# A one-core attention and token-MLP kernel: the first four tiles alone before the first scores, K projected tile by tile, and later slots for the layernorm, FFN and output projection

## The chip, the cores and the metric

The kernel runs on one core of one Trainium2 chip. The metric is device time in microseconds (us) of one execution; lower is better. Engines are named as in the profile: PE is TensorE (matmuls; PEld its weight loads), DVE is VectorE, ACT is ScalarE, POOL is GpSimd, SP is SyncE, which issues the transfers.

## The reference

An input x of 2048 tokens by 512 goes through a layernorm; on it run a multi-head attention (32 heads of 16) and a token-mixing MLP, which mixes over the 2048 tokens with a hidden size of 1376 and has a layernorm of its own. The output is the sum of both and of x.

```python
def _A_ref(x, wqkv, wo):                      # x is layernormed
    qkv = (x @ wqkv).reshape(B, S, 3, H, Dh)  # S 2048, H 32, Dh 16
    scores = einsum("bhqd,bhkd->bhqk", q, k) * Dh ** -0.5
    p = softmax(scores, axis=-1)
    return einsum("bhqk,bhkd->bhqd", p, v) (heads merged) @ wo
def _B_ref(x, w1, b1, w2, b2):
    h = layernorm(x)
    u = gelu(einsum("bsd,sf->bdf", h, w1) + b1)
    return (einsum("bdf,fs->bds", u, w2) + b2) transposed
xn = layernorm(x)
return x + _A_ref(xn, ...) + _B_ref(xn, ...)
```

## The kernel before, in words

**Tiles and blocks.** The tokens lie in 16 tiles of 128. The attention runs in 32 blocks: four blocks of 512 queries (`qb`) by eight groups of four heads (`G`, in pairs: a slice `T` of 128 columns of Q and K and an even or odd half `e`). A block has 16 periods, one per tile of keys. In a period PE computes four score tiles of 128x512 (`score_group`, L664), which row groups of the array hold side by side; ScalarE takes two exps of 128x1024 (`exp_pair`, L673) from PSUM to SBUF as `pT`; two periods later PE multiplies V by `pT` (`pv_group`, L683). A column of ones in V (17 columns per head in the tile `V17`) gives the softmax denominators. At the end of a block `epilogue_copy` (L604) and `task_epilogue_rest` take the sums from PSUM, invert them on DVE (L611, L616) and multiply on POOL (L619) into `oT`.

**Order.** The program writes the instructions of every engine in one fixed order; `Sched` derives the semaphore waits from the keys that an operation reads and writes (`add`, L69). Every engine works strictly in that order. PSUM has eight banks: 0 to 3 (later 0 to 5) hold scores, 6 (`PV_BANK`) the sums, 7 (`EX_BANK`) everything else, one job at a time. Side work gets slots of two units per period (`EXTRA_BUDGET`, L33; a 128x512 matmul is one unit): `sched_list` (L695) gives each job a first period and a rank; `kt`, `qt` and `vt` are the projections of K, Q and V for later slices, `ut` and `yt` the two FFN matmuls, `op` the output projection. Beside this queue, free tasks advance by one step each per period: `epi`, the rest of a block's epilogue, and `ln2`, the second layernorm.

**Prologue.** `pro_stage` (L441) is a pipeline over tiles. A tile goes through `ln_stats` (L326: DVE stats and aggregate, then two small POOL steps that give the inverse deviation), `ln_norm` (L339: DVE), `transpose_pe` (L353), `transpose_copy` (L360: PSUM to `xnT`), `vT_pe` and `vT_evac` (V for slice 0), and every fourth tile `kt_pe` and `kt_evac` (K for slice 0 and 512 keys). Ten stages run ahead of the first scores (`NSTG_PRE = NPRE + 3 + SH`, L465), with ACT for most evictions; the Q projection of slice 0 (`qt_proj`, L392) is in them. The other stages run one per period in block 0, all on DVE. Within a stage the order is eviction, projection, transpose copy, then norm, transpose, then stats of the next tile. `late_consts` (L314) follows the ten stages: POOL clears `wo_pad` (L316), then SP loads it. POOL's `ln_stats` steps queue behind that clear.

The places the change touches in `sched_list`:

```python
for ft in range(NFT):                                              # L704
    sched_list.append((P(1, 4) + 6 * ft, 2, "ut", ft))
for st in range(NT):
    sched_list.append((P(1, 4) + 6 * NFT + 7 * st, 3, "yt", st))
...
        sched_list.append((P(8 * (qb + 1), 8) + 4 * sti, 4, "op", (qb, sti)))
```

`P(b, kt)` is the period of block b and key tile kt.

## Time and profile before

| | |
|---|---|
| time, median of 4 runs | 1021.05 us (1020.63 to 1021.7) |
| profiled execution, its own time | 1020.83 us |
| its span on the core | 1019.0 us |
| busy: ACT / PE / DVE / POOL | 958.7 / 841.2 / 309.6 / 69.3 us |
| mean granted PE clock | 0.775 of full speed |
| chain that ended last | ACT 78%, PE 11%, DVE 7%, POOL 2%, issue 2% |

The profile's busy times are of one execution. A busy PE is not a PE at its peak, since its clock changes and matmuls overlap. Timeline rows give start and length in us from the span's start, engine, line, operation, tiles and, in brackets, the idle time before it with what ended it. Merged rows (x2, x4) show several instructions from the first's start to the last's end.

### The profile page before, as it was taken

The page shows a single profiled execution, that of the slowest core. Times are in us where ns is not written, and L with a number is a line of the kernel's source. Part 1 is how long each engine was busy: PE and PEld are TensorE (multiplying, and loading weights), DVE is VectorE, ACT ScalarE, POOL GpSimd, SP SyncE. Part 2 cuts the span into 40 slices and gives each one's busy share as a digit, 9 for nine tenths or more (in the row PEclk, how much of TensorE's full clock was granted, in tenths as well). Part 3 has the DMA queues.
Part 4 walks back from the last instruction along what each step waited for, and adds up shares of the span by engine and source line. Part 5 has one row for each costly group of instructions (what it writes and reads, how often), then busy time and mean ns, then how long its engine had stood idle before and what let it go on. Part 6 is the DMA issues. An engine that isn't in the chain of part 4 may idle for free.

```text
span 1019.0 us, 11820 instructions
## 1 busy us (share of the span) xinstructions
PE 841.2 (83%) x4957; PEld 205.5 (20%) x5024; DVE 309.6 (30%) x503; ACT 958.7 (94%) x1049; POOL 69.3 (7%) x110
## 2 busy tenths in 40 slices
PE   3786788888788878888888888898989889998986
PEld 1321231231112112212222222211111211111111
DVE  5726632233332243232122323201121321112223
ACT  2595899999999999999999999999999999999995
POOL 2403200000000000000000000000000000000000
PEclk9675998998779787989989999955555965555576
DMA  5030000101100100111100110000000000000000
GB/s 144 19 72 1 1 1 21 22 1 27 36 21 22 21 16 1 28 29 28 33 20 25 29 28 6 16 1 1 0 1 1 16 6 1 1 1 1 1 1 21
DMA packets 55429, 18.33 MB, mean 18 GB/s; under 512 B 49232, under 2 KB 55376, under 8 KB 55376
## 3 DMA queue, kind: packets, MB, share of 16 engines
q1 hardware_dynamic: 55376, 17.58, 7.3%
q8 instruction: 39, 0.64, 0.3%
q14 instruction: 14, 0.11, 0.0%
HBM read 15.47 MB, written 2.10 MB: 17 GB/s over the span
## 4 chain that ended last, share of the span: by engine, by line
ACT 78%; PE 11%; DVE 7%; POOL 2%; issue 2%; another core or an unknown queue 0%; DMA 0%; ACTq 0%; DVEq 0%
ACT pT L673 77%; PE ps L664 4%; PE ps L683 2%; DVE big L345 1%; DVE stats L330 1%; POOL mv L336 1%; PE ps L522 1%; PE ps L400 1%; PE ps L568 1%; DVE QT L408 1%; POOL mv L334 1%; PE ps L382 1%; ACT ga_sb L537 1%; PE ps L549 1%; DVE mv L332 0%
## 5 line engine op out<-in xcount | busy, mean ns | idle before, releaser
L673 ACT ACTIVATE pT<-ps 128x1024 bf16<-128x1024 f32 x1024 | 948.7, 1276 | 26.2 <-PE ps L664 23.4
L664 PE MATMUL ps<-QT,KT 32*128 32x512 bf16 x2048 | 444.2, 478 | 115.7 <-ACT pT L673 96.4
L683 PE MATMUL ps<-pT,V 128*32 128x512 bf16 x2048 | 247.7, 485 | 0.6 <-ACT pT L673 0.6
L664 PEld LDWEIGHTS ps<-QT,KT 32*128 32x128 bf16 x2048 | 92.9, 94 | 502.2 <-ACT pT L673 476.0
L604 DVE COPY OT<-ps 128x512 f32<-128x512 f32 x31 | 21.4, 691 | 325.4 <-PE ps L683 325.4
L616 DVE RECIPROCAL denb<-denb 128x128 f32<-128x128 f32 x124 | 108.6, 920 | 0.9
L619 POOL TENSOR_TENSOR oT<-OT,denb 128x512 bf16<-128x512 f32 x31 | 39.2, 1266 | 837.3 <-DVE denb L616 837.3
L683 PEld LDWEIGHTS ps<-pT,V 128*32 128x32 bf16 x2048 | 52.3, 97 | 154.2 <-issue 152.4
L522 PE MATMUL ps<-big,w1blk 128*128 128x512 bf16 (+1 forms) x158 | 56.8, 435 | 5.6 <-issue 3.7
L549 PE MATMUL ps<-gT,w2blk 128*128 128x512 bf16 (+1 forms) x160 | 54.1, 405 | 3.4 <-DVE QT L408 1.8
L554 DVE SCALAR_TENSOR_TENSOR big<-ps,x_sb 128x512 f32<-128x512 f32 x16 | 11.1, 691 | 108.1 <-PE ps L549 108.1
L568 PE MATMUL ps<-wo_pad,oT 128*128 128x512 bf16 x106 | 38.3, 436 | 3.3 <-issue 2.8
L408 DVE TENSOR_SCALAR QT<-ps,qmask 128x512 bf16<-128x512 f32 x32 | 22.5, 746 | 32.3 <-PE ps L400 30.3
L581 DVE TENSOR_TENSOR osb<-ps,big 128x512 bf16<-128x512 f32 x16 | 11.0, 688 | 58.9 <-PE ps L568 56.8
L400 PE MATMUL ps<-xnT,wqkv_sb 128*128 128x512 bf16 x55 | 24.5, 528 | 4.7 <-DVE KT L390 2.6
L382 PE MATMUL ps<-xnT,wqkv_sb 128*128 128x512 bf16 x55 | 20.7, 464 | 8.8 <-DVE KT L390 5.9
L527 DVE TENSOR_SCALAR u_sb<-ps,b1col 128x512 f32<-128x512 f32 (+1 forms) x11 | 8.2, 748 | 62.0 <-PE ps L522 62.0
L355 PE MATMUL ps<-ident,big 128*128 128x128 bf16 x64 | 8.6, 277 | 16.8 <-DVE big L345 16.7
L611 DVE STREAM_SHUFFLE denb<-OT 128x512 f32<-128x512 f32 x31 | 22.4, 721 | 0.0
L486 PE MATMUL ps<-wqkv_sb,xnT 128*128 128x128 bf16 x192 | 16.1, 232 | 6.1 <-DVE V L390 4.5
L389 ACT ACTIVATE xnT<-ps 128x512 bf16<-128x512 bf16 x8 | 4.8, 597 | 17.0 <-PE ps L355 17.0
L336 POOL TENSOR_TENSOR mv<-mv,mhalf 128x1 f32<-128x1 f32 x32 | 18.1, 567 | 2.7
(52 smaller groups left out, 213.0 us busy)
## 6 DMA issues: line engine op xcount, KB each, us to landing
w1blk<-in_B_w_dram SPq DMA_DIRECT2D x10, 512.0 KB, 4.1
w2blk<-in_B_w_dram SPq DMA_DIRECT2D x16, 320.0 KB, 3.3
out_dram<-osb SPq DMA_DIRECT2D x16, 128.0 KB, 1.7
wqkv_sb<-in_A_wqkv_dram SPq DMA_DIRECT2D x3, 512.0 KB, 6.3
x_sb<-in_A_x_dram SPq DMA_DIRECT2D x3, 512.0 KB, 7.2
wo_pad<-in_A_wo_dram SPq DMA_DIRECT2D x8, 64.0 KB, 2.0
w2blk<-in_B_w_dram SPq DMA_DIRECT2D x16, 24.0 KB, 1.7
w1blk<-in_B_w_dram SPq DMA_DIRECT2D x1, 384.0 KB, 4.0
```

The costliest lines, as they stand in the source:

```text
L336: sc.add("pool", lambda e: e.tensor_tensor(mv[:, i, 2:3], mv[:, i, 1:2], mhalf[:], ALU.pow), reads=[("mv", i), ("mhalf",)], writes=[("mv", ...
L382: sc.add("pe", lambda e, ct=ct: e.matmul(bank(bk), lhsT=wqkv_sb[:, ct, D + 128 * T: D + 128 * T + 128], rhs=xnT[:, ct, 512 * c:512 * (c + ...
L400: sc.add("pe", lambda e, ct=ct: e.matmul(bank(bk), lhsT=wqkv_sb[:, ct, 128 * T:128 * (T + 1)], rhs=xnT[:, ct, 512 * qb:512 * (qb + 1)], st ...
L408: sc.add("dve", lambda e, e_=e_, slot=slot: e.tensor_scalar(QT[:, slot, :], bank(bk), qmask[:, e_:e_ + 1], None, ALU.mult), reads=[("bank" ...
L522: sc.add("pe", lambda e, st=st: e.matmul(bank(EX_BANK)[0:m, :], lhsT=w1blk[:, slot, st, 0:m], rhs=h_sb[:, st, :], start=(st == 0), stop=(s ...
L549: sc.add("pe", lambda e, ft=ft, m=m: e.matmul(bank(EX_BANK), lhsT=w2blk[0:m, slot, ft, :], rhs=gT[0:m, ft, :], start=(ft == 0), stop=(ft = ...
L568: sc.add("pe", lambda e, G=G: e.matmul(bank(EX_BANK), lhsT=oT[:, par, G, 128 * sti:128 * (sti + 1)], rhs=wo_pad[:, G, :], start=(G == 0), ...
L616: sc.add("dve", lambda e, cs=cs: e.reciprocal(denb[:, eb, cs], denb[:, eb, cs]), reads=[("denb", eb, c)], writes=[("denb", eb, c)])
L619: sc.add("pool", lambda e: e.tensor_tensor(oT[:, qb % 2, G, :], OT32[:, eb, :], denb[:, eb, :], ALU.mult), reads=[("OT32", eb)] + [("denb" ...
L664: sc.add("pe", lambda e, r=r, bk=bk: e.matmul(bank(bk), lhsT=KT[32 * r:32 * r + 32, T, 128 * kt:128 * (kt + 1)], rhs=QT[32 * r:32 * r + 32 ...
L673: sc.add("act", lambda e: e.activation(pT[:, buf, :], ps[:, s_ * 1024:(s_ + 1) * 1024], ACTF.Exp, scale=0.25), reads=[("bank", 2 * s_), (" ...
L683: sc.add("pe", lambda e, r=r, buf=buf, off=off: e.matmul(bank(PV_BANK)[32 * r:32 * r + 32, :], lhsT=V17[:, off:off + 32], rhs=pT[:, buf, 5 ...
```

## The change

- `Sched.add`: an operation that reads a PSUM bank now also waits for earlier readers of that bank on other engines.
- The clear of all of `V17` becomes three small clears of the one head per slice that a matmul reads before it is written, one of the end, and the ones.
- `pro_stage` is longer by two steps per tile (norm one stage after stats, transpose one after norm, V two after the copy) and stats of the next tile stand ahead of the norm. Ahead of the first scores only tiles 0 to 3 go all the way (`NSTG_PRE = NPRE + 5`, `SH = 0`), tiles 4 and 5 as far as the norm. There ACT evicts the even half of Q and DVE the odd half.
- In block 0 the K projection of slice 0 is by tile: `kt_tile_pe` and `kt_tile_evac`, 128 keys each, with keys `KTt` by tile for the scores' waits.
- `task_ln2` takes three periods per tile: stats, norm, nothing.
- `ut` and `yt` start at P(4, 2) instead of P(1, 4); the first `w1` loads at P(2, 0) instead of P(0, 8), the first `w2` loads at P(7, 0) instead of P(3, 0).
- `op` of the first three query blocks starts at P(8(qb+1)+6, 2) instead of P(8(qb+1), 8), ahead of FFN jobs that have not started, with the rank of the projections.

```diff
@@ Sched.add
+            if k[0] == "bank":
+                for r in self.readers.get(k, ()):
+                    if r.eng != eng:
+                        deps.add(r)
@@ constants
-        sc.add("dve", lambda e: e.memset(V17[:, :], 0.0), writes=[("Vpad",)] + [("Vone",)] +
-               [("V", t, T) for t in range(NT) for T in range(4)])
+        for T in range(1, 4):
+            sc.add("dve", lambda e, T=T: e.memset(v17_kh[:, :, 8 * T, 0:16], 0.0),
+                   writes=[("V", t, T) for t in range(NT)])
+        sc.add("dve", lambda e: e.memset(V17[:, NKT * H * 17:], 0.0), writes=[("Vpad",)])
@@ K by tile
+        def kt_tile_pe(T, t, bk):
+            j = t % 4
+            for ct in range(NCT):
+                sc.add("pe", lambda e, ct=ct: e.matmul(
+                    bank(bk)[:, 128 * j:128 * (j + 1)], lhsT=wqkv_sb[:, ct, D + 128 * T: D + 128 * T + 128],
+                    rhs=xnT[:, ct, 128 * t:128 * (t + 1)], start=(ct == 0), stop=(ct == NCT - 1)),
+                    reads=[("wqkv", 1), ("xnT", t)], writes=[("bank", bk)])
...
@@ qt_proj_gen
+                if act_first and e_ == 0:
+                    sc.add("act", lambda e, slot=slot: e.activation(QT[:, slot, :], bank(bk), ACTF.Identity,
+                                                                    scale=qmask[:, 0:1]),
...
@@ pro_stage
-        SH = 3
+        SH = 0
...
+            t = s_ - 5
+            if ok(t):
+                vT_evac([t], 0, vb(t), ev if t % 2 == 0 else "dve")
+                if t >= NPRE:
+                    kt_tile_evac(0, t, EX_BANK, "dve")
+                elif t == NPRE - 1:
+                    kt_evac(0, 0, kb(t), ev)
+            t = s_ - 4
+            if ok(t):
+                if t >= NPRE:
+                    kt_tile_pe(0, t, EX_BANK)
+                elif t == NPRE - 1:
+                    kt_pe(0, 0, kb(t))
+                    qt_proj(0, 0, EX_BANK, act_first=True)
+                vT_pe([t], 0, vb(t))
             t = s_ - 3
+            if ok(t):
+                transpose_copy(t, tb(t), ev)
...
-        NSTG_PRE = NPRE + 3 + SH
+        NSTG_PRE = NPRE + 5
@@ task_ln2
-                ln_tile(t, 1)
+                ln_stats(t, 1)
+                yield 0.0
+                ln_norm(t, 1)
+                yield 0.0
@@ score_group
-                    reads=[("KT", T, kt // 4), ("QT", slot_q)], writes=[("bank", bk)], name="sc")
+                    reads=[("KTt", T, kt), ("QT", slot_q)], writes=[("bank", bk)], name="sc")
@@ sched_list and loads
-            sched_list.append((P(1, 4) + 6 * ft, 2, "ut", ft))
+            sched_list.append((P(4, 2) + 6 * ft, 2, "ut", ft))
...
-                    sched_list.append((P(8 * (qb + 1), 8) + 4 * sti, 4, "op", (qb, sti)))
+                    sched_list.append((P(8 * (qb + 1) + 6, 2) + 4 * sti, 0, "op", (qb, sti)))
...
-            if period == P(0, 8):
+            if period == P(2, 0):
...
-            if period == P(3, 0):
+            if period == P(7, 0):
```

DVE at the start of the program, before (`b1c_bf` and `V` are constants; `big` is the normalized x):

```order
L275 MEMSET V 128x4360
L277 MEMSET V 128x512
L330 BN_STATS stats<-x_sb 128x6
L332 BN_AGGR mv<-stats 128x2
L345 TENSOR_SCALAR big<-x_sb,mv 128x512
```

and with the change:

```order
L281 MEMSET V 128x16x8 x3
L283 MEMSET V 128x8
L284 MEMSET V 128x512
L337 BN_STATS stats<-x_sb 128x6
L339 BN_AGGR mv<-stats 128x2
L337 BN_STATS stats<-x_sb 128x6
L339 BN_AGGR mv<-stats 128x2
L352 TENSOR_SCALAR big<-x_sb,mv 128x512
```

The second tile's stats now stand ahead of the first tile's norm, and so on for each tile.

PE around the first scores (scores write `ps` from `QT,KT`; transposes read `ident,big`; V's projection reads `wqkv_sb,xnT`), before:

```order
L382 MATMUL ps<-xnT,wqkv_sb 128x512 x4
L355 MATMUL ps<-ident,big 128x128 x4
L664 MATMUL ps<-QT,KT 128x512 x4
L415 MATMUL ps<-wqkv_sb,xnT 128x128 x4
L355 MATMUL ps<-ident,big 128x128 x4
```

and with the change, from the projections of K and Q on:

```order
L403 MATMUL ps<-xnT,wqkv_sb 128x512 x4
L421 MATMUL ps<-xnT,wqkv_sb 128x512 x4
L441 MATMUL ps<-wqkv_sb,xnT 128x128 x4
L733 MATMUL ps<-QT,KT 128x512 x4
L362 MATMUL ps<-ident,big 128x128 x4
```

A period of block 0 with the change, two periods on (`L752` multiplies V by `pT`):

```order
L733 MATMUL ps<-QT,KT 128x512 x4
L752 MATMUL ps<-pT,V 32x512 x4
L385 MATMUL ps<-xnT,wqkv_sb 128x128 x4
L441 MATMUL ps<-wqkv_sb,xnT 128x128 x4
L362 MATMUL ps<-ident,big 128x128 x4
```

The first scores stand right behind the first four tiles, and every later period of block 0 has a group for K (L385).

DVE in block 1 (`OT` are the block's sums), before:

```order
L390 CAST KT<-ps 128x512
L330 BN_STATS stats<-big 128x6
L332 BN_AGGR mv<-stats 128x2
L345 TENSOR_SCALAR big<-big,mv 128x512
L616 RECIPROCAL denb<-denb 128x128
```

and with the change:

```order
L411 CAST KT<-ps 128x512
L337 BN_STATS stats<-big 128x6
L339 BN_AGGR mv<-stats 128x2
L685 RECIPROCAL denb<-denb 128x128
L352 TENSOR_SCALAR big<-big,mv 128x512
```

Stats and norm of one tile are now a period apart, with other work between them.

## Rows read from the trace of the kernel before

**Rows 1.** The chain that ended last, 580 to 690 us: start, length, what.
```profile
582.46 101.84 ACT pT L673 x111
```

**Rows 2.** ScalarE's timeline, 33 to 120 us: start, length, line, operation [idle before it].
```profile
34.22 1.94 ACT L673 ACTIVATE pT<-ps 128x1024 bf16<-128x1024 f32 x2 [3.38 <-PE ps L664]
...
42.96 1.94 ACT L673 ACTIVATE pT<-ps 128x1024 bf16<-128x1024 f32 x2 [0.37 <-PE ps L664]
...
80.90 4.00 ACT L673 ACTIVATE pT<-ps 128x1024 bf16<-128x1024 f32 x4 [2.61 <-PE ps L664]
```

**Rows 3.** ScalarE's waits, 34.3 to 60, 60 to 115, 115 to 1008: total, times, longest.
```profile
ACT pT L673 <- PE ps L664: 7.5, 6, 3.4
...
ACT pT L673 <- PE ps L664: 12.6, 7, 2.8
...
ACT pT L673 <- PE ps L664: 4.1, 7, 0.8
```

**Rows 4.** DVE's timeline at the start.
```profile
1.73 3.69 DVE L275 MEMSET V<- 128x4360 uint32 x1 [0.87 <-issue]
...
7.35 0.63 DVE L330 BATCH_NORM_STATS2 stats<-x_sb 128x6 f32<-128x512 bf16 x1
8.02 0.18 DVE L332 BATCH_NORM_AGGREGATE mv<-stats 128x2 f32<-128x6 f32 x1
9.20 0.41 DVE L345 TENSOR_SCALAR big<-x_sb,mv 128x512 bf16<-128x512 bf16 x1 [0.99 <-POOL mv L336]
9.52 0.69 DVE L330 BATCH_NORM_STATS2 stats<-x_sb 128x6 f32<-128x512 bf16 x1
```

**Rows 5.** SP's timeline, and the QKV weights' tile: issue to landing.
```profile
5.14 1.18 SPq L265 DMA_DIRECT2D wqkv_sb<-in_A_wqkv_dram  x1
...
DMA to landing us min/median/max: 4.1/6.3/9.1
```

**Rows 6.** Timeline of all engines, from tile 3's norm to Q's eviction.
```profile
15.88 0.41 DVE L345 TENSOR_SCALAR big<-x_sb,mv 128x512 bf16<-128x512 bf16 x1 [0.82 <-POOL mv L336]
...
18.04 1.91 PE L382 MATMUL ps<-xnT,wqkv_sb 128*128 128x512 bf16 x4
...
19.99 0.60 ACT L389 ACTIVATE KT<-ps 128x512 bf16<-128x512 f32 x1 [2.40 <-PE ps L382]
...
21.14 1.41 DVE L408 TENSOR_SCALAR QT<-ps,qmask 128x512 bf16<-128x512 f32 x2 [4.03 <-PE ps L400]
```

**Rows 7.** Timeline of all engines while POOL clears wo_pad.
```profile
33.49 3.55 POOL L316 MEMSET wo_pad<- 128x2048 bf16 x2
...
33.85 0.41 DVE L390 COPY xnT<-ps 128x512 bf16<-128x512 bf16 x1
34.19 3.00 DVE L345 TENSOR_SCALAR big<-x_sb,mv 128x512 bf16<-128x512 bf16 x1
```

**Rows 8.** DVE's timeline in block 0, one tile's V cast and copy.
```profile
49.59 0.26 DVE L390 CAST V<-ps 128x128 bf16<-128x128 f32 x1
49.76 0.41 DVE L390 COPY xnT<-ps 128x512 bf16<-128x512 bf16 x1
```

**Rows 9.** Timeline of all engines in block 1.
```profile
80.25 0.61 PE L664 MATMUL ps<-QT,KT 32*128 32x512 bf16 x4
...
81.36 0.94 DVE L616 RECIPROCAL denb<-denb 128x128 f32<-128x128 f32 x1
...
83.47 0.57 POOL L336 TENSOR_TENSOR mv<-mv,mhalf 128x1 f32<-128x1 f32 x1
...
85.95 1.03 PE L382 MATMUL ps<-xnT,wqkv_sb 128*128 128x512 bf16 x2 [2.47 <-DVE KT L390]
```

**Rows 10.** Stretches: length, busy time (instructions) of each engine, PE clock, DMA, GB/s.
```profile
40.00:45.00 5.00, 4.92 (x32) 2.26 (x33) 3.77 (x13) 4.08 (x5) 1.80 (x5) 0.57 0.13 39
45.00:50.00 5.00, 4.28 (x46) 1.83 (x43) 4.16 (x12) 4.11 (x5) 1.58 (x4) 1.00 0.10 28
200.00:600.00 400.00, 333.56 (x2079) 83.63 (x2113) 122.70 (x180) 395.70 (x434) 16.45 (x13) 0.89 0.10 22
```

More of the change, by code (lines that the diff above doesn't have):

```diff
@@ L371, in kt_evac, with kt_tile_evac @@
         def kt_evac(T, c, bk, evac_eng):
-            evac(evac_eng, KT[:, T, 512 * c:512 * (c + 1)], bank(bk), reads=[("bank", bk)], writes=[("KT", T, c)])
+            evac(evac_eng, KT[:, T, 512 * c:512 * (c + 1)], bank(bk), reads=[("bank", bk)],
+                 writes=[("KTt", T, t) for t in range(4 * c, 4 * c + 4)])
+        def kt_tile_pe(T, t, bk):
[5 more added lines that the diff above has]
+                    reads=[("wqkv", 1), ("xnT", t)], writes=[("bank", bk)])
+        def kt_tile_evac(T, t, bk, evac_eng):
+            j = t % 4
+            evac(evac_eng, KT[:, T, 128 * t:128 * (t + 1)], bank(bk)[:, 128 * j:128 * (j + 1)],
+                 reads=[("bank", bk)], writes=[("KTt", T, t)])
         def kt_pe(T, c, bk):
@@ L390, in evac, with qt_proj, qt_proj_gen @@
             return sc.add("dve", lambda e: e.tensor_copy(dst, src), reads=reads, writes=writes)
-        def qt_proj(qb, T, bk):
-            for _ in qt_proj_gen(qb, T, bk):
+        def qt_proj(qb, T, bk, act_first=False):
+            for _ in qt_proj_gen(qb, T, bk, act_first):
                 pass
-        def qt_proj_gen(qb, T, bk):
+        def qt_proj_gen(qb, T, bk, act_first=False):
             for ct in range(NCT):
@@ L469, in block0_work, with pro_stage_late @@
         def block0_work(period):
-            pro_stage(period + NSTG_PRE, False)
+            s_ = period + NPRE + 2
+            if s_ < NSTG_PRE:
+                pro_stage_late(s_)
+            else:
+                pro_stage(s_, False)
+        def pro_stage_late(s_):
+            for d_, fn in ((5, None), (4, None), (3, None), (2, None)):
+                pass
+            t = s_ - 5
+            if NPRE <= t < NT:
+                vT_evac([t], 0, vb(t), "dve")
+                kt_tile_evac(0, t, EX_BANK, "dve")
+            t = s_ - 4
+            if NPRE <= t < NT:
+                kt_tile_pe(0, t, EX_BANK)
+                vT_pe([t], 0, vb(t))
+            t = s_ - 3
+            if NPRE <= t < NT:
+                transpose_copy(t, tb(t), "dve")
+            t = s_ - 2
+            if NPRE <= t < NT:
+                transpose_pe(t, tb(t))
+            t = s_
+            if NPRE + 2 <= t < NT:
+                ln_stats(t, 0)
+            t = s_ - 1
+            if NPRE + 2 <= t < NT:
+                ln_norm(t, 0)
         def task_ln2():
@@ L567, in task_outproj @@
                 yield 1.0
+                assert cur_period[0] <= P(8 * (qb + 2) + 1, 0), "out-projection too late: o^T already recycled"
                 sc.add("pe", lambda e, G=G: e.matmul(
@@ L692, in P @@
             return b * NKT + kt
+        cur_period = [0]
         sched_list = []
@@ L788, in bass_parallel_sum__softmax_full_mha__mixer_token_mlp__prompt_kernel @@
                 tk_new = Task(kind, arg, start_task(kind, arg))
-                if kind in ("qt", "kt", "vt"):
+                if kind in ("qt", "kt", "vt", "op"):
                     pos_ins = 1 if bank_q and bank_q[0].started else 0
-                    while pos_ins < len(bank_q) and bank_q[pos_ins].kind in ("qt", "kt", "vt"):
+                    while pos_ins < len(bank_q) and bank_q[pos_ins].kind in ("qt", "kt", "vt", "op"):
                         pos_ins += 1
```

36 lines of the change are left out of this document (16 added, 20 removed).

## The prediction

> **What bounds the kernel now.** I read the timeline of ScalarE first, then its waits by stretch, then DVE, PE, POOL and SP at the places where ScalarE stands idle. ScalarE runs 1,024 exps of 128x1024. In a stretch where nothing else ends last, 111 of them take 101.84 us [rows 1], 0.9175 us each, so all of them need 939.5 us. The first starts at 34.22 us [rows 2], and the span is 1019.0 us. Three things therefore lie around a fixed core: the time to the first exp, the holes between exps, and the end (about 11 us from the last exp, which the change leaves as it is). Holes are waits of an exp for its scores on PE [rows 3]. The first of the three stretches gives 7.5 us, of which 3.4 are the wait before the first exp, so 4.1 in block 0 proper; the second, mostly block 1, 12.6; the third, the whole rest, 4.1. Each break also leaves its run of exps longer than the pitch: the four exps from 80.90 took 4.00 us, not 3.67 [rows 2]. With six such runs in block 1 that is 2.0 more, 14.6 in all there. The eleven tanh of the FFN on ScalarE stay eleven.
>
> All sums are made against the profiled execution, 1020.83 us (span 1019.0 and 1.83 around it), which lies 0.22 under the median of 1021.05. A measurement of this kernel can tell about 0.2%, 2.0 us, from no change.
>
> **Start to the first exp.** Now ten stages run ahead of the first scores: nine tiles are normalized, eight of them carried to their V. After the change six are normalized and four carried to V. In the old order one tile is a serial chain on DVE: stats, aggregate, POOL's two small steps, norm, next stats, 2.17 us from one stats to the next (7.35 to 9.52 [rows 4]). The new order puts the next tile's stats between, so DVE no longer waits for POOL: from the same rows stats to aggregate 0.67, the aggregate's own 0.18, norm to stats 0.32, some 1.17 per tile. The 3.69 us memset of V [rows 4] becomes five small ones.
>
> What is late next is a load. The Q weights are issued at 5.14 us and their landing is the longest of that tile's, 9.1 us [rows 5]: 14.24 us. The fourth norm comes before that: the old first stats at 7.35 could move to 3 to 5 us, and the fourth norm is 5.4 us behind it (1.85 from the first stats to its norm, three more at 1.17), so about 10; K's projection then starts 2.16 us after it (15.88 to 18.04 [rows 6]), near 12, and is done when the Q weights land. From 14.24: the Q projection's four matmuls take what K's took to its eviction, 1.95 us (18.04 to 19.99 [rows 6]); then ScalarE evicts Q and K one after the other, 0.60 each [rows 6]; then 0.65 from scores to exp (80.25 [rows 9] to 80.90 [rows 2]). That is 18.04 us, against 34.22: **16.2 us gained**. Ends: 17.4 (TensorE at the upper clock halfway through) and 19.8. The latter holds if the first stats stay at 7.35: fourth norm 12.75, K's projection 14.9, Q's eviction 3.10 later as now (18.04 to 21.14 [rows 6]), 18.0, then the same 1.85 to the exp.
>
> In this stretch POOL clears wo_pad after the sixth tile instead of the tenth. Before, that clear ran 3.55 us from 33.49, and a norm of 0.41 us started beside it took 3.00, while a copy from PSUM took its usual 0.41 [rows 7]. In the new DVE order the norm of tile 5 would be the one held, until about 15.5 us; behind it stand the odd-head eviction of Q, which waits for ScalarE's read of the same bank until about 16.8 anyway, and V's of tile 3 (0.26 us [rows 8]), needed by the second half of the first scores. They end near 17.8, and the second exp is due at 18.96. So the clear costs nothing in its new place. Its cover is the wait for the Q weights; without it, the second exp would be late by up to the 2.6 us that the old norm lost.
>
> **Block 0.** Twelve tiles instead of eight are left for its 16 periods (one group of scores, two exps, 1.84 us each). Per period PE gets four K matmuls of 128 columns where it had four of 512 every fourth period, and DVE gets a K cast of 128 columns, in price like V's cast. DVE's starts follow each other at 0.17 (V: 49.59 to 49.76 [rows 8]), 0.17 (K), 0.34 (copy: 33.85 to 34.19 [rows 7]), 0.67, 0.18, 0.32: about 1.85 us, just the pace of the exps. PE decides by its clock, of which the rows show two levels, 1.2 and 2.4 GHz. At the lower clock the old period took 2.31 us (exps of 1.94 and a hole of 0.37 [rows 2]) with PE busy 4.92 of 5.00 us (40 to 45 us, granted 0.57 [rows 10]); another group of four 128-column matmuls, 0.4 there, makes 2.7, or 0.87 lost per period. At the upper clock (45 to 50 us, granted 1.00 [rows 10]) 46 matmuls took 4.28 us, so the 20 of a new period take 1.86: next to nothing lost. The old block 0 went through about three periods of the first kind. I take three, 2.6, and 1.7 for the start (the pipeline has two tiles in hand when the scores begin, where it had several): 4.3 against 4.1, **0.2 lost**. Bounds: 1.5 us of holes, or all twelve periods slow, 11.2.
>
> **Block 1.** The holes there come from PE, which waits up to 2.47 us for DVE's eviction of K [rows 9]. DVE is late since every period holds a whole second layernorm tile, with about 1 us of waiting for POOL between its two halves (0.99 [rows 4]), and a reciprocal of 0.94 [rows 9]. After the change a tile is spread over three periods: stats, norm in the next, then nothing. Two periods of DVE then hold one eviction (0.6), two reciprocals (1.8) and two thirds of a tile (1.17 x 2/3 = 0.8): 3.2 us against 3.67 of exps, where it was 0.6 + 1.8 + 2 x 2.2 = 6.8. On average DVE keeps up; what stays is a reciprocal in front of an eviction now and then, three or four times up to 0.94. I leave 3.1 of the 14.6: **11.5 gained**, between 8 and 13.5. The layernorm now ends in block 3, before its reader, the FFN, which starts in block 4.
>
> **FFN and output projection.** The same matmuls in the same slots of two a period, later: by the order of instructions the first FFN matmul comes after 81 groups of scores (53 before), the last after 318 of 512 (304). The first w1 loads on SP move from period 8 to 32, so they lead their reader by 49 periods instead of 45; the first w2 loads move from 48 to 112, 87 ahead of theirs. The wo_pad loads ahead of them start earlier, when the clear is done. The third output projection moves next to the fourth, so the last two blocks carry 56 such matmuls (24 before). The last sits in period 510, where it was 506; its residual add is one DVE step and ends before the tail's shuffle. From 200 to 600 us, with work of this kind in most periods, ScalarE was busy 395.70 of 400 [rows 10], so 28 crowded periods cost little: **0.5 lost**, bounds 0 and 2. The added waits between readers of one bank bind only at the eviction of Q, counted above.
>
> **Sum.** 1020.83 - 16.2 + 0.2 - 11.5 + 0.5 = **993.8 us**.
>
> **A rule against it.** The held norm [rows 7] shows that a POOL instruction can block a DVE one. The Trainium skill (SBUF — State Buffer, "SBUF: two separate sides") says DVE in a two-port mode and GpSimd take a shared port pair as an exclusive lock, whoever starts first holding it for its whole instruction. The rows agree on the lock, not on its length: 3.00 us spans both clears. In block 0 each of twelve norms could meet POOL's steps for another tile. My sum has nothing for it: in the new order the norm of one tile starts as the next tile's aggregate ends, and POOL's steps for that tile wait for that aggregate too, so the norm comes first, if narrowly. If every norm lost POOL's longer step, 0.57 [rows 9], the sum would be 993.8 + 6.8 = 1000.6.
>
> **Rivals.**
> - TensorE stays at 1.2 GHz through block 0: 11.2 us of holes, 1000.7. For it: from 40 to 45 us PE was busy 98% and still low [rows 10]. Against: it then rose, and the new block is denser. 12%.
> - DVE still ends last in block 1, with half of the 14.6 left: 998.0; with all, 1005.3. For: DVE's 3.2 of 3.67 is tight, and PE takes its slots in order. 8%.
> - The lock in block 0, 1000.6. Against: the steps are short. 4%.
> - The early memset is not what delays the first stats, so the start is not shortened as it says: first exp at 19.8, 995.6. 2%.
> - Slower: the FFN at TensorE's low clock. Place: its 176 periods of two matmuls. Price: scores and P·V 0.61 each and two matmuls 1.03 [rows 9] are 2.25 us, 0.41 over two exps, at most 72 us. It beats the 27.0 gained, and 2.0 more, from 71 such periods on: 1066 with all. Against: the granted clock was 0.89 where the same work runs now [rows 10]. 3%.
>
> **How the numbers follow.** My case has 71%. Its best ends (first exp 17.4, block 0 at 1.5, block 1 at 13.5, nothing lost late) give 988; I go to 987. Upwards the range takes in the slow block 0, half the stalls of block 1 and the lock, with a late first exp on one of them: 1003. Left out: two of these together, and the last rival. Only that one reaches no change or slower: faster 0.97, same 0.01, slower 0.02.
>
> **What would show it.** Right: first exp near 18 us, after the landing of the Q weights; wait of exps in block 1 under 4 us; stats of the second layernorm without POOL's wait behind them. Wrong: a first exp after 20, periods of 2.7 us beyond the fifth in block 0, evictions of K that PE waits on for over 2 us, or a granted clock near 0.5 through the FFN with holes between exps.

## The result and the profile after

The changed kernel takes **985.48 us** (median of 8 runs, 983.75 to 987.52) against 1020.83 for the kernel before (median of 13, 1019.17 to 1022.86): a ratio of 0.9652, 95% interval 0.9642 to 0.9663, 35.4 us less. The forecast was 993.8 us with a range of 987 to 1003. The direction was right and the gain 8 us too small; the median lies 1.5 us under the range. The profiled execution took 986.67 us, its span 984.5.

The profile page of the changed kernel: busy times, the granted clock in 40 slices, the chain that ended last, and the exp's group (busy and mean ns, idle before and its main releaser).

```profile
PE 830.7 (84%) x4995; PEld 207.1 (21%) x5060; DVE 307.3 (31%) x520; ACT 954.2 (97%) x1044; POOL 70.2 (7%) x110
...
PEclk9989959988978888889999999555965555555797
...
ACT 84%; PE 12%; DVE 2%; issue 1%; DMA 1%; SPq 0%; ACTq 0%
...
L742 ACT ACTIVATE pT<-ps 128x1024 bf16<-128x1024 f32 x1024 | 946.6, 1402 | 7.0 <-PE ps L733 4.8
```

The engines' busy times are those of before within 11 us. What went is idle time: ScalarE is now busy 97% of the span, and VectorE and GpSimd, 7% and 2% of the old chain, are 2% and nothing. ScalarE's timeline of the changed kernel, from the eviction of Q on, answers to [rows 2]; [ ] holds the idle time before a row:

```profile
16.24 0.69 ACT L430 ACTIVATE QT<-ps,qmask 128x512 bf16<-128x512 f32 x1 [4.51 <-PE ps L421]
...
18.12 5.66 ACT L742 ACTIVATE pT<-ps 128x1024 bf16<-128x1024 f32 x6 [0.70 <-PE ps L733]
25.07 1.94 ACT L742 ACTIVATE pT<-ps 128x1024 bf16<-128x1024 f32 x2 [1.29 <-PE ps L733]
27.57 30.69 ACT L742 ACTIVATE pT<-ps 128x1024 bf16<-128x1024 f32 x32 [0.56 <-PE ps L733]
58.58 88.44 ACT L742 ACTIVATE pT<-ps 128x1024 bf16<-128x1024 f32 x96 [0.32 <-PE ps L733]
```

The first exp starts at 18.12 us instead of 34.22. From 58.58 on, 96 exps run without a break where the old kernel had seven holes [rows 3]. The waits by stretch, 14 to 60 and 115 to 974 us (from 60 to 115 there is none):

```profile
ACT pT L742 <- PE ps L733: 2.9, 4, 1.3
...
ACT pT L742 <- PE ps L733: 1.9, 5, 0.6
```

Waits leave out that exps in a short run take longer, so the rest of this text counts the **loss**: from the trace, the start of one exp to the start of a later one, less 0.9175 us [rows 1] for each exp between. Block 0 is exps 0 to 32, block 1 is 32 to 64; with the two behind it, 32 to 66 takes in all of the old holes. The stretch "66 on" contains the eleven tanh in every kernel.

| profiled execution | first exp | loss 0-32 | 32-66 | 66 on | own time |
|---|---|---|---|---|---|
| before | 34.22 | 5.2 | 14.6 | 13.9 | 1020.83 |
| after | 18.12 | 2.9 | 0.5 | 11.6 | 986.67 |
| difference | -16.1 | -2.3 | -14.1 | -2.3 | -34.2 |

What is left to -34.2 (0.7 the other way) lies behind the last exp and around the span.

### The profile page after: what moved, and what is told of

It reads as the page before. It is cut to its first block, busy times and chain, and to the rows that moved or that the text cites. A ratio compares the mean times of both kernels' runs of the same rounds, so it can differ in the third digit from the quotient of the medians.

```text
span 984.5 us, 11908 instructions
## 1 busy us (share of the span) xinstructions
PE 830.7 (84%) x4995; PEld 207.1 (21%) x5060; DVE 307.3 (31%) x520; ACT 954.2 (97%) x1044; POOL 70.2 (7%) x110
## 4 chain that ended last, share of the span: by engine, by line
ACT 84%; PE 12%; DVE 2%; issue 1%; DMA 1%; SPq 0%; ACTq 0%
ACT pT L742 83%; PE ps L733 4%; PE ps L752 3%; PE ps L590 1%; PE ps L421 1%; DMA wqkv_sb<-in_A_wqkv_dram 1%; PE ps L403 1%; ACT ga_sb L605 1%; DVE QT L434 0%; SPq L269 0%; PE ps L617 0%; DVE denb L702 0%; PE ps L637 0%; PE ps L385 0%; DVE osb L650 0%
## 5 line engine op out<-in xcount | busy, mean ns | idle before, releaser
L733 PE MATMUL ps<-QT,KT 32*128 32x512 bf16 x2048 | 450.0, 470 | 120.0 <-ACT pT L742 99.4
L752 PE MATMUL ps<-pT,V 128*32 128x512 bf16 x2048 | 242.5, 474 | 1.0 <-ACT pT L742 1.0
L733 PEld LDWEIGHTS ps<-QT,KT 32*128 32x128 bf16 x2048 | 95.0, 94 | 505.4 <-ACT pT L742 480.5
L752 PEld LDWEIGHTS ps<-pT,V 128*32 128x32 bf16 x2048 | 52.2, 97 | 149.6 <-issue 147.3
L637 PE MATMUL ps<-wo_pad,oT 128*128 128x512 bf16 x107 | 34.7, 397 | 2.4 <-issue 1.7
L434 DVE TENSOR_SCALAR QT<-ps,qmask 128x512 bf16<-128x512 f32 x31 | 21.9, 746 | 33.7 <-PE ps L421 32.5
L421 PE MATMUL ps<-xnT,wqkv_sb 128*128 128x512 bf16 x53 | 24.1, 534 | 3.6 <-issue 2.8
L411 DVE CAST V<-ps 128x128 bf16<-128x128 f32 (+1 forms) x26 | 12.4, 476 | 28.9 <-PE ps L554 22.3
L403 PE MATMUL ps<-xnT,wqkv_sb 128*128 128x512 bf16 x46 | 18.1, 477 | 2.8 <-issue 1.3
L590 PEld LDWEIGHTS ps<-big,w1blk 128*128 128x128 bf16 (+1 forms) x176 | 10.7, 102 | 28.7 <-issue 24.6
L617 PEld LDWEIGHTS ps<-gT,w2blk 128*128 128x128 bf16 (+1 forms) x176 | 10.7, 98 | 25.3 <-issue 22.9
```

The source lines that it names most:

```text
L403: sc.add("pe", lambda e, ct=ct: e.matmul(bank(bk), lhsT=wqkv_sb[:, ct, D + 128 * T: D + 128 * T + 128], rhs=xnT[:, ct, 512 * c:512 * (c + ...
L421: sc.add("pe", lambda e, ct=ct: e.matmul(bank(bk), lhsT=wqkv_sb[:, ct, 128 * T:128 * (T + 1)], rhs=xnT[:, ct, 512 * qb:512 * (qb + 1)], st ...
L434: sc.add("dve", lambda e, e_=e_, slot=slot: e.tensor_scalar(QT[:, slot, :], bank(bk), qmask[:, e_:e_ + 1], None, ALU.mult), reads=[("bank" ...
L590: sc.add("pe", lambda e, st=st: e.matmul(bank(EX_BANK)[0:m, :], lhsT=w1blk[:, slot, st, 0:m], rhs=h_sb[:, st, :], start=(st == 0), stop=(s ...
L617: sc.add("pe", lambda e, ft=ft, m=m: e.matmul(bank(EX_BANK), lhsT=w2blk[0:m, slot, ft, :], rhs=gT[0:m, ft, :], start=(ft == 0), stop=(ft = ...
L637: sc.add("pe", lambda e, G=G: e.matmul(bank(EX_BANK), lhsT=oT[:, par, G, 128 * sti:128 * (sti + 1)], rhs=wo_pad[:, G, :], start=(G == 0), ...
```

## The experiments

All times are medians, with the ratio to the kernel before on the same chip and its 95% interval. Theory A and B in the recorded expectations are two accounts of what the edit should show.

**1 to 4: which part gave what.** Edits: (1) the old kernel with only the second layernorm split over two periods; (2) the changed kernel with the whole tile in one period again; (3) the changed kernel with the old slots of the FFN, output projection and weight loads, and a layernorm tile over two periods; (4) the same with the whole tile, so that only the new start is left.

```
 # (1), in the kernel before
-                ln_tile(t, 1)
+                ln_stats(t, 1)
+                yield 0.0
+                ln_norm(t, 1)
 # (2), in the changed kernel
-                ln_stats(t, 1)
-                yield 0.0
-                ln_norm(t, 1)
-                yield 0.0
+                ln_tile(t, 1)
 # (3) and (4), slots back, two of seven lines
-sched_list.append((P(4, 2) + 6 * ft, 2, "ut", ft))
+sched_list.append((P(1, 4) + 6 * ft, 2, "ut", ft))
-            if period == P(2, 0):
+            if period == P(0, 8):
```

> The kernel before with one part of the change: the second layernorm's stats in one period, its norm in the next (two periods per tile, so that it still ends before the FFN of the old slots). Theory A (block 1's holes come from stats, POOL's wait and norm standing in one period, and from nothing else): the waits of exps between 60 and 115 us fall from 12.6 to under 2, first exp stays at 34.2, time 1006 to 1009. Rival B (the holes go only with the new start, since K by tile or TensorE's clock decides): the waits stay above 8, time above 1016.

> The changed kernel with the second layernorm whole in one period again, all else as changed. Theory A: block 1 gets its holes back, 11 to 13 us of waits between 52 and 105 us, time 998 to 1001, first exp still at 18.1. Rival B: no holes, time under 990.

> The changed kernel with the FFN, the output projection and the weight loads in their old slots (second layernorm two periods per tile, so that it ends before the FFN). Theory A (the later slots took about 2 us of waits out of the part behind block 1, chiefly where a Q projection fell between FFN matmuls): waits behind 105 us rise from 1.9 to about 4, time 987 to 989. Rival B (the later slots do nothing): 985 to 986. Rival C (the old slots collide with the second layernorm): above 991.

> The kernel before with the new start alone: memsets, four tiles ahead of the scores, K by tile in block 0; second layernorm whole, slots old. Theory A (the three parts add up): first exp at 18.1, block 0 with about 2.2 us of waits, block 1 with its 11 to 13, time 1002 to 1005. Rival B (the start collides with block 1, and gives part of its gain back there): above 1007.

| run | time | ratio | first exp | loss 0-32 | 32-66 | 66 on |
|---|---|---|---|---|---|---|
| (1) layernorm split alone | 1004.75 | 0.9845 (0.9823 to 0.9866) | 34.80 | 6.0 | -0.1 | 11.4 |
| (2) layernorm whole | 999.93 | 0.9803 (0.9779 to 0.9828) | 17.94 | 2.7 | 13.9 | 11.6 |
| (3) old slots | 986.64 | 0.9666 (0.9648 to 0.9684) | 18.16 | 2.7 | -0.5 | 13.2 |
| (4) start alone | 1000.04 | 0.9801 (0.9782 to 0.9821) | 17.34 | 3.3 | 15.6 | 12.3 |

ScalarE's waits from 52 to 115 us, of run (1) and of run (2):

```profile
ACT pT L675 <- PE ps L666: 0.3, 1, 0.3
```

```profile
ACT pT L739 <- PE ps L730: 12.6, 7, 3.5
```

Three lines in the old kernel take the holes of block 1 away, and taking them out of the changed kernel brings them back, 12.6 us as before [rows 3]. The split is worth 16.4 us in the old kernel (1021.14 to 1004.75) and 14.4 in the new (999.93 to 985.48). The new start by itself is worth 21.1 (1021.14 to 1000.04), some microseconds more than its share of the table above. The slots are worth nothing that can be told: (3) and the changed kernel overlap, and so do (2) and (4), which differ by the slots alone. Theory A held for (1), (2) and (4) in its mechanism, though (1) and (4) took 1.3 and 2.0 us less than it said; (3) lies between its theories, and its waits behind 105 us are 2.7 where theory A said about 4.

**5: amount of work, or the wait for GpSimd?** The old holes have two readings: too much VectorE work per period, or VectorE waiting about 1 us in the middle of a tile for GpSimd's two small steps (1.0 of [rows 4]). VectorE's wait in the old kernel from 60 to 115 us:

```profile
DVE big L345 <- POOL mv L336: 13.9, 14, 1.0
```

This edit keeps a whole tile's work in a period but takes the two halves from different tiles:

```
-            for t in range(NT):
-                yield 0.0
-                ln_stats(t, 1)
-                yield 0.0
-                ln_norm(t, 1)
-                yield 0.0
+            for t in range(NT + 1):
+                yield 0.0
+                if t < NT:
+                    ln_stats(t, 1)
+                if t > 0:
+                    ln_norm(t - 1, 1)
```

> The changed kernel, but LayerNorm 2 takes 17 periods of block 1 instead of 32: each has the statistics of one tile and the normalisation of the tile before, so the amount of VectorE work in a period is that of the old kernel (1.25 us beside the evictions), while no normalisation stands behind GpSimd's step of the same period. Theory A (the holes of block 1 come from VectorE waiting for GpSimd inside a period, and from the eviction that queues behind that wait): no loss in exps 42 to 66 (under 1 us over the 0.9175 us pitch), 984 to 987 us. Theory B (it is the amount of VectorE work in a period): the losses come back, 6 to 12 us of them, 991 to 998 us.

Measured: 984.45 us, 0.9651 (0.9636 to 0.9666); loss 1.4 over exps 32 to 66, 0.5 of it from 42 on. Two stretches of this run (length, busy time of PE, PEld, DVE, ACT, POOL, granted clock, DMA, GB/s) and VectorE's rows of one tile:

```profile
58.00:68.00 10.00, 7.52 (x59) 2.06 (x56) 9.83 (x21) 9.58 (x11) 4.66 (x10) 1.00 0.00 0
68.00:78.00 10.00, 8.37 (x84) 3.71 (x82) 9.72 (x24) 9.78 (x11) 5.67 (x14) 1.00 0.01 2
```

```profile
62.91 0.68 DVE L337 BATCH_NORM_STATS2 stats<-big 128x6 f32<-128x512 bf16 x1
63.62 0.18 DVE L339 BATCH_NORM_AGGREGATE mv<-stats 128x2 f32<-128x6 f32 x1
63.72 0.38 DVE L352 TENSOR_SCALAR big<-big,mv 128x512 bf16<-128x512 bf16 x1
64.02 0.95 DVE L685 RECIPROCAL denb<-denb 128x128 f32<-128x128 f32 x1
```

VectorE is busy 98% of the time here (9.83 and 9.72 of 10 us), and ScalarE still runs. So the holes came from the wait in the middle of the tile, which kept the evictions behind it from starting; a whole tile's work per period does not make them by itself. The old kernel's stretch, from 78 to 98 us, for comparison, and then the changed kernel's:

```profile
78.00:88.00 10.00, 5.91 (x29) 1.06 (x30) 6.91 (x14) 4.61 (x6) 2.37 (x6) 0.52 0.01 2
88.00:98.00 10.00, 6.33 (x34) 1.06 (x30) 6.91 (x14) 6.97 (x8) 3.60 (x7) 0.50 0.00 0
```

```profile
78.00:88.00 10.00, 8.55 (x74) 3.25 (x76) 6.58 (x14) 10.00 (x12) 1.58 (x4) 1.00 0.00 0
88.00:98.00 10.00, 8.47 (x53) 2.12 (x52) 6.94 (x11) 10.00 (x13) 2.81 (x5) 1.00 0.01 2
```

Before, no engine was busy for more than 7 of 10 us: VectorE waited for GpSimd, PE for VectorE, ScalarE for PE. PE, idle so often, was granted 0.5 there, 1.2 GHz; now it is granted 1.00, 2.4 GHz, and VectorE has as many busy microseconds as before. The low clock went with the holes, so how much of the 14 to 16 us is the wait itself and how much PE's slower matmuls behind it, no run separates.

**6 to 9: what bounds the new start.** Edits of the changed kernel: (6) the Q weights' load moved ahead of tiles 8 to 15; (7) GpSimd's clear of `wo_pad` moved out of the start, in eight pieces, to periods 68 to 75, its loads to period 78; (8) the clear moved to period 6 of block 0; (9) the old single memset of `V17`.

```
 # (6)
         ld_w(1)
+        ld_w(0)
         ld_x(8, 12)
         ld_x(12, 16)
-        ld_w(0)
 # (7), late_consts keeps only its two casts
+            if 68 <= period < 76:
+                late_clear(period - 68)
+            if period == 78:
+                late_wo()
 # (8)
+            if period == 6:
+                late_clear(0)
+                late_clear(1)
+                late_wo()
 # (9), instead of four memsets
+        sc.add("dve", lambda e: e.memset(V17[:, :], 0.0), ...
```

> The changed kernel with the load of the Q weights ahead of the loads of x tiles 8 to 15. Theory A (the landing of the Q weights at 14.3 us is what ends last before the first exp): the Q projection starts behind K's, at 13.4, and the first exp comes 0.9 us earlier, near 17.2; time 0.5 to 1 below the changed kernel's, 984.5 to 985. Rival B (the clear of wo_pad or ScalarE's evictions end last): first exp stays at 18.1.

> The changed kernel with the clear of wo_pad taken out of the start: eight pieces, one per period from period 68 on, and the loads behind them. Theory A (the clear is hidden behind the wait for the Q weights): the norm of tile 5 takes its 0.41 us instead of 3.61, first exp still at 18.1, second still 0.9 behind it, time unchanged, 984.5 to 986.5. Rival B (the held norm costs something on the path): the time falls by over 1 us.

> The changed kernel with the clear of wo_pad in period 6 of block 0, where nothing covers it. Theory A (POOL's clear holds a DVE norm, and all behind it on DVE, as before the change): one norm of about 3 us, a hole of 1.5 to 3 us in block 0 beside the 2.2 of now, time 987 to 988.5. Rival B (the pipeline in block 0 has enough in hand to take a hold of 3 us): holes in block 0 unchanged, time under 986.5.

> The changed kernel with the clear of all of V by one memset, as before. Theory A (that memset sets the first stats, and then the order of DVE, not the landing of the Q weights, sets the first scores): first stats at 7.3 instead of 3.1, the fourth norm near 12.7, first exp at 19.5 to 20.2, time 1.4 to 2.1 above the changed kernel's, 987 to 987.6. Rival B (the memset was hidden behind the loads): first exp under 18.6.

| run | time | ratio | first exp | loss 0-42 | first exp + loss |
|---|---|---|---|---|---|
| changed kernel | 985.48 | 0.9652 (0.9642 to 0.9663) | 18.12 | 3.8 | 21.9 |
| (6) Q weights first | 983.27 | 0.9641 (0.9624 to 0.9658) | 16.81 | 2.7 | 19.5 |
| (7) clear late | 984.13 | 0.9641 (0.9622 to 0.966) | 17.09 | 2.2 | 19.3 |
| (8) clear in block 0 | 986.91 | 0.9669 (0.965 to 0.9689) | 18.15 | 4.3 | 22.5 |
| (9) old memset | 984.72 | 0.9654 (0.9635 to 0.9673) | 18.78 | 2.2 | 21.0 |

(6) bears out that the Q weights' landing sets the first exp: 1.3 us earlier, where 0.9 was expected.

(8) shows the price of the clear where nothing covers it. Its VectorE norm, GpSimd's two memsets, and ScalarE:

```profile
31.80 2.91 DVE L355 TENSOR_SCALAR big<-x_sb,mv 128x512 bf16<-128x512 bf16 x1
```

```profile
31.02 3.55 POOL L326 MEMSET wo_pad<- 128x2048 bf16 x2
```

```profile
36.37 1.94 ACT L745 ACTIVATE pT<-ps 128x1024 bf16<-128x1024 f32 x2 [1.62 <-PE ps L736]
39.05 31.46 ACT L745 ACTIVATE pT<-ps 128x1024 bf16<-128x1024 f32 x34 [0.74 <-PE ps L736]
```

The norm is held through both memsets, as in [rows 7], and two holes of 2.4 us together follow. Other losses of the changed kernel are missing in turn: the sum of them is only 0.6 us above the changed kernel's, and the intervals of the two times overlap. With the clear gone from its place in the start (7) the norm that it held takes 0.41 us, so it is the clear that holds it. In the start nothing waits for that norm; the first exp of (7), 1.0 us earlier than expected, has another reason, the next point. The median of (7) is 1.4 us lower, by theory B's measure, but its interval overlaps the changed kernel's.

(9) was expected at 19.5 to 20.2 us by the theory that the earlier statistics set the start, and under 18.6 by its rival. It came between, 18.78. Its Q projection:

```profile
16.06 1.03 PE L419 MATMUL ps<-xnT,wqkv_sb 128*128 128x512 bf16 x4
```

With the statistics 4.2 us later (7.35 instead of 3.12) the Q projection starts 1.74 us later (14.32 before) and no longer waits for its weights: here VectorE's order sets the start, as the theory says. The four matmuls took 1.03 us instead of 1.89, which gives about half of it back, so the first exp comes 0.66 us later; the time shows nothing of it.

**10 to 12: PE's clock at the start.** The Q projection's four matmuls took 1.89 us in the changed kernel, but 1.04 in (7), and also in (4) and (5), whose start is the changed kernel's own, with the clear in its place. PE's row of run (4):

```profile
14.39 1.04 PE L421 MATMUL ps<-xnT,wqkv_sb 128*128 128x512 bf16 x4 [1.01 <-DMA wqkv_sb<-in_A_wqkv_dram]
```

So it is no work of the clear: the level at that place differs between executions of the same start. The edits: (10) two matmuls with no reader while PE waits for the Q weights and two while it waits for the evictions of Q and K; (11) edits (6) and (7) together; (12) those and two such matmuls.

```
                     kt_pe(0, 0, kb(t))
+                    for i in range(NFILL1):
+                        filler()
                     qt_proj(0, 0, EX_BANK, act_first=True)
                 vT_pe([t], 0, vb(t))
+                if pre and t == NPRE - 1:
+                    for i in range(NFILL2):
+                        filler()
```

> The changed kernel with four more 128x512 matmuls whose result nobody reads: two between the K and the Q projection, where TensorE waits for the Q weights, and two behind the V matmuls that follow the Q projection, where it waits for the evictions of Q and K. Theory A (block 0 still loses time because TensorE comes into it at the lower clock, for which its idle stretches before are the reason): the Q projection takes near 1.04 us for its four matmuls instead of 1.89, the two long periods of 2.49 us go, first exp at 17.1 to 17.6, loss over exps 0 to 42 at most 2 us instead of 3.75, 982 to 984 us. Theory B (the low level there does not hang on these idle stretches, or block 0 is held by its chain of evictions): Q projection 1.8 to 1.9 us, first exp 18.0 to 18.6, loss 3 to 4, 985 to 987 us.

> Both small edits that gave shorter medians by themselves: the Q weights loaded ahead of the tiles 8 to 15, and the clear of the padded output weights taken out of the start (eight pieces in periods 68 to 75). Theory A (they shorten different waits): first exp at 16.2 to 16.6, loss over exps 0 to 42 near 2.2 us, 981 to 983 us. Theory B (each of the two medians is the same as the changed kernel's within its spread): 983 to 986 us.

> The same two edits and two filling matmuls behind the V matmuls that follow the Q projection, where TensorE waits for the evictions of Q and K. Theory A (clock at the start of block 0): the first periods of block 0 run at the higher clock, loss over exps 0 to 42 at most 1.5 us, first exp at 16.2 to 16.6, 980 to 982 us. Theory B (no effect of the filling): as without it, 981 to 986 us.

| run | time | ratio | first exp | loss 0-42 | first exp + loss |
|---|---|---|---|---|---|
| (10) filled | 985.50 | 0.9654 (0.9639 to 0.967) | 18.63 | 3.8 | 22.5 |
| (11) Q first, clear late | 984.57 | 0.9645 (0.963 to 0.9661) | 16.26 | 4.8 | 21.1 |
| (12) both and filled | 983.75 | 0.9639 (0.9624 to 0.9654) | 16.15 | 4.8 | 21.0 |

PE's timeline of run (10), and its stretches from 20 us:

```profile
15.89 1.04 PE L421 MATMUL ps<-xnT,wqkv_sb 128*128 128x512 bf16 x4 [0.72 <-DMA wqkv_sb<-in_A_wqkv_dram]
...
22.33 0.60 PE L362 MATMUL ps<-ident,big 128*128 128x128 bf16 x4 [1.32 <-DVE xnT L411]
```

```profile
20.00:22.00 2.00, 0.48 (x4) 0.09 (x2) 0.99 (x4) 2.00 (x3) 0.00 (x0) 0.92 0.04 12
22.00:24.00 2.00, 1.67 (x13) 0.61 (x14) 1.97 (x6) 0.89 (x2) 1.53 (x4) 0.50 0.12 33
24.00:26.00 2.00, 2.00 (x20) 1.36 (x16) 1.77 (x7) 1.45 (x2) 0.97 (x3) 0.50 0.12 33
26.00:28.00 2.00, 2.00 (x21) 1.32 (x20) 1.29 (x5) 1.94 (x2) 0.85 (x2) 0.50 0.16 45
```

With the filling the Q projection takes 1.04 us, but (4) and (5) have that without it, so the run does not show that the filling did it. For block 0 it does nothing: PE then does little for some microseconds (0.48 of 2.00 us at 20 to 22), falls to 0.50, and has its long periods there instead. In (11) and (12) the start gains 1.9 us, the loss grows by 1.1, and the time moves by 1 to 2. (In the profiled execution of (10) everything from the fourth tile's transposes on ran about 1 us later, K's projection at 12.64 instead of 11.71, so its first exp tells nothing of the filling.) In all three PE stands idle for `xnT`, a copy of VectorE, until 20.8 to 22.3 us, also where the first exp came at 16.2. The reason stands in VectorE's timeline; this is the changed kernel's:

```profile
17.91 0.16 DVE L330 CAST b1col<-b1c_bf 128x11 f32<-128x11 bf16 x1
19.14 0.17 DVE L331 CAST b2col<-b2c_bf 128x16 f32<-128x16 bf16 x1 [1.07 <-DMA b2c_bf<-in_B_b_dram]
19.23 0.69 DVE L337 BATCH_NORM_STATS2 stats<-x_sb 128x6 f32<-128x512 bf16 x1
```

Two casts of bias columns end the start. In the old order their loads, small but slow to issue, had long landed; in the new one VectorE waits for the second until 19.1 us (19.5 to 21.0 in the three), and everything of block 0 queues behind.

An early first exp is given back in unchanged starts too. In six executions with the changed kernel's own start, runs (2) to (5), the changed kernel and (13), the first exp comes from 17.22 to 18.16 us, and first exp and loss over exps 0 to 32 together are 20.6 to 21.0 in all six.

**13 to 16: the casts out of the way.** (13) is the changed kernel again, on the chip of (14) to (16); (14) moves the two casts to period 40; (15) does so with edits (6) and (7); (16) adds the two filling matmuls.

```
+            if period == 40:
+                late_cast()
```

> The changed kernel once more, on the same chip as the other three of this call, as their measure. Both theories: 985 to 986 us, first exp 18.1, loss over exps 0 to 42 of 2.6 to 3.8 us over the 0.9175 us pitch.

> The changed kernel with the two casts of the bias columns moved from the end of the start to period 40. Theory A (VectorE waits for the bias loads in front of them until 19.1 us, and block 0 queues behind): the statistics that started at 19.23 start near 18.0, no wait for the bias loads is left, TensorE stays busier in the first periods, loss over exps 0 to 42 at 1.5 to 2.5 us instead of 3.75; 983.5 to 984.5 us. Theory B (the lower clock holds block 0 by itself): first exp and loss unchanged, 985 to 986 us.

> Q weights first, clear of the padded output weights late, and the casts late. Theory A: first exp at 16.2 to 16.6 as with the first two edits, and the wait of 2.1 us for TensorE at 20 to 22 us goes: loss over exps 0 to 42 at 1.5 to 2.5 us instead of 4.8, 980.5 to 982.5 us. Theory B: the loss stays at 4 to 5 us, 983 to 985 us.

> The same with two filling matmuls behind the V matmuls after the Q projection. Theory A: TensorE, at the higher level from the Q projection on and no longer left idle at 18 to 21 us, stays at it: no period of 2.49 us, loss over exps 0 to 42 under 1.5 us, 980 to 982 us. Theory B: two long periods stay, loss 2.5 to 5 us, 982 to 985 us.

| run | time | ratio | first exp | loss 0-42 | first exp + loss |
|---|---|---|---|---|---|
| (13) changed kernel again | 986.09 | 0.9651 (0.9631 to 0.967) | 17.94 | 3.3 | 21.2 |
| (14) casts late | 985.16 | 0.9647 (0.9624 to 0.967) | 18.13 | 2.2 | 20.4 |
| (15) Q first, clear and casts late | 983.87 | 0.9637 (0.9616 to 0.9659) | 16.85 | 2.2 | 19.0 |
| (16) the same and filled | 983.58 | 0.9628 (0.9611 to 0.9645) | 16.71 | 2.3 | 19.1 |

VectorE and the stretches of run (15):

```profile
16.86 0.68 DVE L340 BATCH_NORM_STATS2 stats<-x_sb 128x6 f32<-128x512 bf16 x1
```

```profile
16.00:18.00 2.00, 1.18 (x10) 0.49 (x10) 1.97 (x5) 1.51 (x3) 0.16 (x1) 1.00 0.53 2
18.00:20.00 2.00, 1.47 (x10) 0.55 (x10) 1.25 (x4) 2.00 (x3) 1.47 (x4) 0.59 1.11 215
20.00:22.00 2.00, 1.85 (x11) 0.48 (x12) 1.51 (x4) 2.00 (x3) 0.58 (x3) 0.50 1.35 219
```

The statistics that started at 19.23 start at 16.86, neither the wait for the loads nor PE's wait for `xnT` is left, and the loss falls from 4.8 in (11) to 2.2, first exp and loss together from 21.1 to 19.0. So the casts did make PE wait in (11) and (12). How much of the 2.0 us is theirs is not shown: (6) and (7), with the casts in their place, have sums of 19.5 and 19.3, and there PE was granted 1.00 again from 26 and 24 us on, in (11) only from 28. In the changed kernel itself (14) the loss is 2.2 instead of 3.8 and 3.3, as theory A said, but the time cannot be told from that of (13). All three of (14) to (16) took longer than theory A said, by 0.7 us and more. Nor are the theories cleanly parted: in (15) PE still falls to 0.50 near 19 us, after a stretch in which it was busy 1.18 of 2.00 us, in (16) too with the filling, and one stretch at 1.2 GHz at the start of block 0 remains in each of (10) to (16), in (13) by the durations of its matmuls.

The medians of the five kernels that load the Q weights early are 983.27 to 984.57, under both medians of the changed kernel (985.48, 986.09) by 1 to 3 us. Each single interval overlaps the changed kernel's, so no one of them is shown faster by itself. (16) has the lowest ratio.

## Why the prediction missed

**Start: right.** Forecast 18.04 us for the first exp from the landing of the Q weights; measured 18.12, 16.1 us gained for 16.2. That the number fits to 0.1 is in part luck: the forecast took the Q projection at 1.95 us, and where it ran at 1.04, in (4) and (5), the same start has its first exp at 17.34 and 17.22. The rows that should show it (VectorE's first statistics and its held norm, then PE):

```profile
3.12 0.63 DVE L337 BATCH_NORM_STATS2 stats<-x_sb 128x6 f32<-128x512 bf16 x1
...
12.20 3.61 DVE L352 TENSOR_SCALAR big<-x_sb,mv 128x512 bf16<-128x512 bf16 x1 [0.56 <-POOL mv L343]
```

```profile
11.71 1.86 PE L403 MATMUL ps<-xnT,wqkv_sb 128*128 128x512 bf16 x4 [0.35 <-ACT xnT L410]
14.32 1.89 PE L421 MATMUL ps<-xnT,wqkv_sb 128*128 128x512 bf16 x4 [0.75 <-DMA wqkv_sb<-in_A_wqkv_dram]
```

K's projection was put "near 12", the weights at 14.24; they are 11.71 and 14.32. The norm that the clear would hold "until about 15.5" is held to 15.8, and the clear "costs nothing in its new place": nothing waits for it (run 7).

**Block 1: right in its place, too small by 2.6.** "I leave 3.1 of the 14.6" failed; 0.5 is left. The step was the load of two periods, "one eviction (0.6), two reciprocals (1.8) and two thirds of a tile", 3.2 of 3.67 us. That holds for a few periods only. VectorE's groups of the changed kernel from 58 to 119 us (busy, mean ns, idle before and its releaser):

```profile
L685 DVE RECIPROCAL denb<-denb 128x128 f32<-128x128 f32 x9 | 8.3, 929 | 0.0
L337 DVE BATCH_NORM_STATS2 stats<-big 128x6 f32<-128x512 bf16 x12 | 8.1, 674 | 0.0
L352 DVE TENSOR_SCALAR big<-big,mv 128x512 bf16<-128x512 bf16 x11 | 6.3, 576 | 3.7 <-POOL mv L343 3.7
L411 DVE CAST V<-ps 128x512 bf16<-128x512 f32 x8 | 5.5, 691 | 10.4 <-PE ps L554 10.4
L411 DVE CAST KT<-ps 128x512 bf16<-128x512 f32 x7 | 4.8, 680 | 5.8 <-PE ps L403 5.8
```

There are nine reciprocals in 33 periods, where the step counted one in each: the whole kernel has 124, four in each block of 16 periods, which stand in a few periods close together. And in front of its evictions VectorE now waits for PE (16.2 us in these two groups), not PE for VectorE. In the same stretch PE waits for a K eviction once:

```profile
PE ps L733 <- ACT pT L742: 7.2, 27, 0.5
...
PE ps L403 <- DVE KT L411: 0.4, 1, 0.4
```

So the term that failed is the 1.8 for the reciprocals. By the step's count run (5) needs 0.6 + 1.8 + 2 x 1.25 = 4.9 us of VectorE in 3.67, and it has next to no holes. With the right number, 0.5 for the reciprocals of two periods on average, the same sum gives about 1.9 for the changed kernel, 3.6 for run (5), about what its 98% say, and 5.5 for the old kernel, where 2.0 are the two waits for GpSimd: they are what does not fit, and nothing is left when they go. That a reciprocal would often stand in front was a guess from one row [rows 9], and the upper bound of the gain, 13.5, was too low for the same reason; 14.1 came.

**Block 0: wrong by 2.5.** Forecast 0.2 lost; measured 2.3 gained. Of the error 1.1 is the measure: 4.1 of the old block were waits alone, the new periods were counted as loss; by loss the old block had 5.2. The other 1.4 is "I take three" long periods at 2.7 us and 1.7 for the start. Two were long, of 2.5 us (PE's P·V rows of the changed kernel start at 22.48, 24.97 and 27.56), and from then PE all but kept pace: the 32 exps from 27.57 took 30.69 us, 0.96 each. The three were taken over from the old block, which "went through about three periods of the first kind": a count and no mechanism. In both profiled executions of the changed kernel, this and (13), the loss over exps 0 to 32 is 2.9. What the forecast did not see at all, the wait for the bias loads, is not what made the number wrong: it can only make the time longer, and the forecast was too long. Nor is the bound of 11.2 for twelve slow periods the forecast's own 12 x 0.87, which is 10.4; the rival built on it would stand at 999.9 instead of 1000.7.

**FFN and output projection: forecast 0.5 lost, measured 2.3 less in the profiled pair.** The runs do not tie this to the slots: with the old ones the loss from exp 66 on was 11.4 to 13.2 in runs (1), (3) and (4), with the new ones 9.2 to 13.7. The old profiled execution (13.9) lies just above that spread. What sets it from one execution to the next stays open. So does the 1.2 us between the profiled difference (34.2) and that of the medians (35.4).

**The other rivals** did not occur. PE was at the upper level from 27.56 us on, within block 0; PE waited for VectorE's K eviction for 0.4 us in block 1; the first statistics came at 3.12 us; and from 200 to 400 and 400 to 600 us, where the FFN runs, PE was granted 0.84 and 0.97 (0.86 and 0.92 before) and ScalarE was busy 198.7 and 198.8 of 200 us. Behind the FFN, from 690 us on, the clock is 0.65 (0.60 before), and ScalarE is busy 283.1 of 284 us.

**The rule on the shared port.** Nor did the lock in block 0: the ten norms there (the forecast counted twelve) take 0.38 to 0.40 us. Where a norm does meet the clear, 3.61 us at the start and 2.91 in run (8) against 0.41 without it, the rows agree with the Trainium skill (SBUF — State Buffer, "SBUF: two separate sides") that one engine's instruction locks the other out. They again show a hold over two instructions: 3.61 us, where each of the two memsets takes 1.80.

**Sum.** The start gave 0.1 less than forecast; block 0 was 2.5, block 1 2.6 and the rest 2.8 too pessimistic, 0.7 behind the last exp the other way: 7.1 us between 993.8 and the profiled 986.67. The three errors have one sign. In block 1 a leftover was put down for a wait that the change removes; in block 0 three long periods were taken over from the old block, and two came; for the third, 2.8, no cause is shown. The range's lower end was built by adding the good ends of the same terms, so it fell short with them, by 1.5 us.

## What to carry to other kernels

Where an engine waits in the middle of a short chain for another one, and in-order work stands behind it, put the two halves into different steps: three lines were worth 14 to 16 us, and the engine may even be busy nearly all the time afterwards. Before adding an instruction into a period's load, count how often it occurs (four reciprocals in a block stood in the sum as sixteen), and if the wait that makes the holes goes, do not leave a share of them for safety. When a start is shortened, look for the small late loads whose readers end it: covered before, they can make an engine wait at a time that no longer depends on the start. Here that wait is shown, a gain in time from its removal is not.
